# Two key weight loads moved to ScalarE's DMA queue, and two value weight loads moved ahead of the fifth token tile's load

## The chip, the cores and the metric

The kernel runs on one core of a Trainium2 chip. The metric is device time in microseconds (us) of one execution. A kernel's executions agree to a few tenths of a per cent, so every ratio is given with its 95% interval. The "span" of a profile runs from its first to its last instruction and is about 1.7 us shorter than the time of the same execution.

## The reference, cut to what matters

```python
x = A_x                                       # 2048 tokens of 448 numbers
h = x + A(layernorm(x), A_wqkv, A_w_phi, A_wo)
h2 = h + B(layernorm(h), B_w_gate, B_w_up, B_w_down)

def A(x, wqkv, w_phi, wo):                    # linear attention, 16 heads of 28
    q, k, v = split(x @ wqkv)
    pk = einsum("bhsd,hdf->bhsf", k, w_phi)   # the same w_phi for q
    ...
```

The kernel never forms k: it multiplies the key weights by w_phi once (the "fold") and projects each normalised token tile with the product. So the first projection needs three things: token tiles 0 and 1, normalised and transposed; all key weights; and w_phi. The value weights are needed one step later.

## The kernel before

Every operation has a name, and for each engine a string gives the order in which that engine runs its operations. Waits on semaphores are worked out from what the operations read and write.

```python
ORDER = {
    "sp":  "x1 x0 ld_k0 x2 ld_k2 x4 x6 ld_v0 x10 ld_v2 ld_q2 x8 ld_q3 ..."       # cut
    "act": "wphi3 wphi2 wphi1 wphi0 wTe1 wTe0 wTe3 w2e0_0 w2e0_1 w2e0_2 w2e0_3 xn3 ..."
    "pe":  "warm0 wT1 wT0 warm1 xT1 warm2 xT0 warm3 wT2 wT3 w2m0_0 warm4 w2m0_1 "
           "w2m0_3 w2m0_2 warm5 xT2 warm6 ppa0 warm7 ppb0 xT3 vva0 vvb0 ppa2 ..."
    "dve": "zero bd0 bst1 agg1 bst0 agg0 ve1_0 nm1_0 nm1_1 xn1 bst2 bst3 agg2 agg3 ve1_3 "
           "xT0e wTe2 bst5 nm1_3 bst4 agg5 agg4 bst6 xT1e ve1_4 ..."
    "pool": "... ve1_1 pow1_1 pow1_0 xn0 v1ones mask1 nm1_2 ve1_2 pow1_2 nb1_2 xn2 ..."
}
# ... cut ...
def kload(a, b):      # two of the four key weight blocks, 196 KB
    load("ld_k%d" % a, wk_sb[:, a:b, :], A_wqkv[a * GP:b * GP, D:2 * D]..., [...], (b - a) * 98)
# ... cut ...
load("wphi%d" % hl, Wphi[...], ..., [("Wphi", hl)], 6, r=["Wphi"], eng="act")    # after bd0 zeroed the tile
```

`x1` and `x0` load one token tile each (112 KB), `x2`, `x4`, `x6`, ... two tiles each (224 KB); `ld_v0` and `ld_v2` are the value weights (224 KB each). `bst` are a tile's statistics on VectorE (DVE), `xn` the normalisation, `xT` its transposition on TensorE (PE), `xTe` the copy out of PSUM. `wT` transposes key weights, `w2m0` is the fold (the key weights by w_phi) and `w2e0` its copies; `ppa0` is the first key projection and `vva0` the first value projection. The `warm` groups are multiplications of zeros that fill TensorE until data comes.

The softmax here doesn't subtract the row's maximum and nothing guards it: scores larger than these inputs give would overflow.

Of the kernel before, what the change touches and what calls it, by code (L numbers as in the profile page):

```python
# [18 lines left out]
class Graph:  # L19
# [86 lines left out]
    def emit(self, nc):  # L106
# [94 lines left out]

ORDER = {
    "sp": (
        "x1 x0 ld_k0 x2 ld_k2 x4 x6 ld_v0 x10 ld_v2 ld_q2 x8 ld_q3 ld_q1 ld_q0 xT4 xT5 xT6 x14 x12 xT7 ld_woe1 xT8 "
        "xT9 xT10 xT11 xT12 xT13 xT14 ld_woo1 xT15 ld_wd0 ld_woe0 ld_wu2 ld_wg0 ld_wg2 ld_wd1 ld_wg3 ld_wu3 ld_woo0 "
        "ld_wu0 ld_wg1 ld_wd4 ld_wd6 ld_wu1 oT3 oT2 oT4 oT5 oT6 oT7 hT2 ld_wd3 ld_wd2 hT3 ld_wd5 hT4 oT8 oT9 hT5 hT6 "
        "hT7 oT11 oT10 oT12 out3 out1 hT9 hT8 oT13 hT11 hT10 oT14 oT15 out5 hT12 hT14 out2 hT15 out4 hT13 out9 out7 "
        "out10 out6 out14 out0 out15 out12 out11 out8 out13 "
    ),
    "act": (  # L210
        "wphi3 wphi2 wphi1 wphi0 wTe1 wTe0 wTe3 w2e0_0 w2e0_1 w2e0_2 w2e0_3 xn3 xn4 ek0 ek1 xn5 v1_0 v1_1 xn6 ek2 ek3 "
        "v1_2 w2e1_1 v1_3 xn7 ek4 w2e1_3 xn9 w2e1_2 ek5 v1_5 v1_6 ek6 xn11 ek7 xn12 ek8 v1_8 xn13 ek9 xn14 ek10 v1_10 "
        "ek11 v1_11 ek12 v1_12 ek13 v1_13 ek14 eq0_0 ek15 v1_14 v1_15 eq0_1 eq1_0 eq1_1 eq2_0 oT0e eq2_1 sq0 sq1 "
        "eq3_0 eq3_1 sig0_1 sig0_0 sig0_3 sig0_2 sig0_5 sig0_4 sig0_7 sq2 sig0_6 sq3 sig0_9 sig0_8 sig0_10 sig0_11 "
        "sq5 sig0_12 sig0_13 sq4 sq7 sig2_0 sig2_1 sq6 sig2_3 sig2_2 sig2_5 sig2_4 sig2_6 sig2_7 sig2_8 sig2_9 "
        "sig2_10 sig2_11 sig2_12 sig2_13 sig4_1 sq9 sig4_0 sig4_3 sq8 sig4_2 sig4_5 sig4_4 sig4_7 sig4_6 sig4_9 sq10 "
        "sig4_8 sq11 sig4_11 sig4_10 sig4_13 sig4_12 sig8_1 sig8_0 sq13 sig8_2 sig8_3 sig8_4 sig8_5 sq12 sig8_6 sq14 "
        "sq15 sig8_7 sig8_9 sig8_8 sig8_10 sig8_11 sig8_13 sig8_12 sig12_0 sig12_1 sig12_3 sig12_2 sig12_5 sig12_4 "
        "sig12_7 sig12_6 sig12_8 sig12_9 sig12_11 sig12_10 sig12_12 sig12_13 "
    ),  # L220
    "pe": (
        "warm0 wT1 wT0 warm1 xT1 warm2 xT0 warm3 wT2 wT3 w2m0_0 warm4 w2m0_1 w2m0_3 w2m0_2 warm5 xT2 warm6 ppa0 warm7 "
# [83 lines left out]
def build(nc, A_x, A_wqkv, A_w_phi, A_wo, B_w_gate, B_w_up, B_w_down, out):  # L306
# [10 lines left out]
    with ExitStack() as es:  # L317
# [69 lines left out]
        def load(name, dst, src, w, kb, r=(), eng="sp"):  # L387
            return op(eng, name, lambda e: e.dma_start(dst, src), r=r, w=w, dma="in" if eng == "sp" else "ain",  # L388
                      nring=48 if eng == "sp" else 8, kb=kb)
# [34 lines left out]

        def kload(a, b):
            load("ld_k%d" % a, wk_sb[:, a:b, :], A_wqkv[a * GP:b * GP, D:2 * D].rearrange("(kt p) n -> p kt n", p=GP),
                 [("wk", kt) for kt in range(a, b)], (b - a) * 98)

        def vload(k):
            r0 = ROW0[k]  # L430
            load("ld_v%d" % k, wv_sb[:, k:k + 2, :], A_wqkv[r0:r0 + 256, 2 * D:3 * D].rearrange("(kt p) n -> p kt n", p=P),
                 [("wv", k), ("wv", k + 1)], 224)
        kload(0, 2)
        kload(2, 4)
        for hl in range(4):
            load("wphi%d" % hl, Wphi[hl * DH:(hl + 1) * DH, :, hl * DH:(hl + 1) * DH],
# [98 lines left out]
        for kt in range(KT):  # L535
            b = (0, 1, 4, 5)[kt]
# [351 lines left out]
```

## Time and profile before

| | before |
|---|---|
| time, median of 3 runs | 208.53 us (207.93 to 208.68) |
| span of the profiled run | 206.8 us |
| TensorE busy | 199.2 us, 96% of the span |
| first key projection starts | 10.59 us |

Three lines of the page of the kernel before: busy time, share and instructions of each engine, and the shares of the chain that ended last, by engine and by line.

```profile
PE 199.2 (96%) x2457; PEld 112.6 (54%) x2457; DVE 136.6 (66%) x343; ACT 95.2 (46%) x185; POOL 59.0 (29%) x99
...
PE 86%; DVE 4%; POOL 3%; DMA 2%; issue 1%; ACT 1%; SPq 1%
PE psum L289 79%; PE psum L814 5%; DMA x_sb<-in_A_x_dram 2%; POOL o_pad L700 1%; PE psum L478 1%; POOL rst L728 1%; SPq L388 1%; DVE hn_pad L732 1%; DVE st L485 1%; ACT eq L637 0%; PE psum L553 0%; ACT eq L638 0%; POOL xn_pad L514 0%; PE psum L464 0%; DVE hhT L788 0%
```

TensorE bounds the kernel: it is busy for 96% of the span and carries 86% of the chain.

Stretches of the span of the same kernel (columns: length, then the busy time and count of PE, of its weight loads, of DVE, ACT and POOL, the granted clock, the DMA share and rate):

```profile
0.00:10.59 10.59, 9.15 (x86) 6.02 (x87) 7.33 (x26) 4.56 (x8) 6.64 (x24) 1.00 0.84 225
...
13.00:30.00 17.00, 16.80 (x232) 9.63 (x230) 16.53 (x36) 16.54 (x35) 14.57 (x18) 1.00 0.44 98
...
100.00:150.00 50.00, 49.99 (x526) 24.14 (x522) 31.87 (x77) 18.89 (x39) 7.59 (x18) 1.00 0.22 43
```

In the first 10.59 us TensorE counts as busy for 9.15 us, but most of that is zeros. From 13 us on it has nearly no gap, so whatever delays the first projection should delay the end.

TensorE's timeline of the head (start us, duration, engine, line, operation, tiles, count; in brackets the idle time before it and what ended it):

```profile
1.24 4.02 PE L464 MATMUL psum<-zero 128*128 128x512 bf16 x9 [1.24 <-DVE zero L392]
5.22 0.99 PE L540 MATMUL psum<-ident,wk_sb 112*112 112x112 bf16 x8
...
6.90 0.39 PE L478 MATMUL psum<-ident,xn_pad 128*128 128x128 bf16 x4
...
7.59 0.36 PE L553 MATMUL psum<-Wphi,WkT 112*128 112x112 bf16 x4
...
9.76 0.40 PE L478 MATMUL psum<-ident,xn_pad 128*128 128x128 bf16 x4 [0.20 <-POOL xn_pad L514]
...
10.59 0.93 PE L289 MATMUL psum<-Wk,xnT 64*128 64x448 bf16 x8
...
12.73 1.55 PE L289 MATMUL psum<-wv_sb,xnT 64*128 64x448 bf16 x12
```

(The last row counts only what starts before 14 us, the end of the window.) These are, in order: the first warm-up group, the first key transposes, tile 0's transpose, the first fold group, tile 2's transpose, the first key projection and the first value projection. The only stop between them is 0.20 us, for tile 2's normalisation on GpSimd (POOL).

VectorE's timeline of the same stretch: statistics of tile 1, of tiles 2 and 3, of tile 5, then the copy of tile 1's transpose, without which the first projection cannot start:

```profile
2.88 0.63 DVE L485 BATCH_NORM_STATS2 st<-x_sb 128x6 f32<-128x448 bf16 x1 [1.46 <-DMA x_sb<-in_A_x_dram]
...
6.05 1.15 DVE L485 BATCH_NORM_STATS2 st<-x_sb 128x6 f32<-128x448 bf16 x2 [0.58 <-DMA x_sb<-in_A_x_dram]
...
8.15 0.62 DVE L485 BATCH_NORM_STATS2 st<-x_sb 128x6 f32<-128x448 bf16 x1
...
10.00 0.41 DVE L471 COPY xnT<-psum 128x512 bf16<-128x512 bf16 x1
```

The first of them waited for tile 1 (landed 2.1 us after its issue at 0.79), the second for tiles 2 and 3. The piece of the chain of waits that stands for the load of tiles 2 and 3 (start us, length, what):

```profile
2.17 3.85 DMA x_sb<-in_A_x_dram
```

From there the chain runs over VectorE's statistics and over GpSimd to tile 2's normalisation, which ends at 9.71 us, just before tile 2's transpose.

### The profile page before, as it was taken

How to read it: one execution, taken by the hardware profiler on the slowest of the kernel's cores; microseconds unless marked ns; L12 is line 12 of the kernel's file. 1: busy time of each engine (PE TensorE's matmuls, PEld its weight loads, DVE VectorE, ACT ScalarE, POOL GpSimd, SP SyncE). 2: the span in 40 equal slices, each digit the busy share in tenths (PEclk: the TensorE clock that was granted, in tenths of full speed). 3: DMA queues.
4: the chain of work that ended last, by engine and by line, in shares of the span. 5: the costliest groups of instructions: out<-in, count | busy, mean ns of one | idle time of the engine just before them, and what ended most of it. 6: DMA issues, size and time to landing. Idle time of an engine off the chain costs nothing.

```text
span 206.8 us, 5794 instructions
## 1 busy us (share of the span) xinstructions
PE 199.2 (96%) x2457; PEld 112.6 (54%) x2457; DVE 136.6 (66%) x343; ACT 95.2 (46%) x185; POOL 59.0 (29%) x99
## 2 busy tenths in 40 slices
PE   7999999999989999999999999999999999999991
PEld 2935666775446666777444444444555555544450
DVE  4899999978899897767768967446332513353151
ACT  2689999878792536222333342324323122122100
POOL 4868999831345404400032020001400000000000
PEclk9999999999999999999999999999999999999997
DMA  5945344899122270413005411030321000020013
GB/s 156 292 107 135 82 95 88 247 382 258 56 51 54 44 166 32 79 25 55 3 0 91 109 29 25 15 41 22 78 49 25 3 0 3 0 89 3 0 37 119
DMA packets 32722, 16.25 MB, mean 79 GB/s; under 512 B 24952, under 2 KB 31800, under 8 KB 32696
## 3 DMA queue, kind: packets, MB, share of 16 engines
q1 hardware_dynamic: 32192, 15.86, 31.2%
q8 instruction: 19, 0.31, 0.6%
q10 hardware_dynamic: 504, 0.03, 0.2%
q14 instruction: 7, 0.06, 0.1%
HBM read 8.34 MB, written 1.84 MB: 49 GB/s over the span
## 4 chain that ended last, share of the span: by engine, by line
PE 86%; DVE 4%; POOL 3%; DMA 2%; issue 1%; ACT 1%; SPq 1%
PE psum L289 79%; PE psum L814 5%; DMA x_sb<-in_A_x_dram 2%; POOL o_pad L700 1%; PE psum L478 1%; POOL rst L728 1%; SPq L388 1%; DVE hn_pad L732 1%; DVE st L485 1%; ACT eq L637 0%; PE psum L553 0%; ACT eq L638 0%; POOL xn_pad L514 0%; PE psum L464 0%; DVE hhT L788 0%
## 5 line engine op out<-in xcount | busy, mean ns | idle before, releaser
L289 PE MATMUL psum<-xnT,wg_sb 64*128 64x512 bf16 (+1 forms) x490 | 94.6, 333 | 0.7 <-DVE qq L685 0.6
L289 PE MATMUL psum<-xnT,wu_sb 64*128 64x512 bf16 (+1 forms) x490 | 94.5, 334 | 0.3
L787 ACT ACTIVATE sg_sb<-psum 128x512 bf16<-128x512 f32 (+1 forms) x70 | 35.0, 512 | 89.9 <-PE psum L289 89.4
L788 DVE SCALAR_TENSOR_TENSOR hhT<-sg_sb,psum 128x512 bf16<-128x512 bf16 (+1 forms) x70 | 39.1, 576 | 50.8 <-ACT sg_sb L787 50.3
L289 PEld LDWEIGHTS psum<-xnT,wg_sb 64*128 64x128 bf16 x490 | 43.8, 94 | 23.7 <-DVE hhT L788 4.8
L289 PEld LDWEIGHTS psum<-xnT,wu_sb 64*128 64x128 bf16 x490 | 43.9, 94 | 15.1 <-PE psum L289 1.4
L289 PE MATMUL psum<-wd_sb,hhT 64*128 64x448 bf16 x336 | 37.2, 349 | 0.0
L289 PEld LDWEIGHTS psum<-wd_sb,hhT 64*128 64x128 bf16 x336 | 17.3, 94 | 14.8 <-DVE x_sb L718 0.6
L607 POOL TENSOR_TENSOR phi<-hhT,rs 128x896 bf16<-128x896 bf16 x13 | 22.7, 1770 | 2.6 <-DVE rs L604 1.5
L289 PE MATMUL psum<-wv_sb,xnT 64*128 64x448 bf16 x112 | 22.0, 350 | 0.1
L289 PE MATMUL psum<-Wk,xnT 64*128 64x448 bf16 x112 | 22.0, 350 | 0.1
L726 POOL TENSOR_SCALAR ve<-ssq 128x1 f32<-128x1 f32 x16 | 3.1, 192 | 61.2 <-ACT junk L723 60.4
L603 DVE TENSOR_REDUCE ss<-hhT 128x32 f32<-128x896 bf16 x16 | 17.0, 1070 | 1.2 <-ACT hhT L600 1.1
L700 POOL TENSOR_TENSOR o_pad<-c_sb,rden 128x448 bf16<-128x448 bf16 x12 | 11.2, 937 | 19.0 <-DVE rden L695 17.4
L289 PE MATMUL psum<-xnT,Wq 64*120 64x512 bf16 x112 | 14.7, 381 | 0.2
L289 PE MATMUL psum<-wo_e,oT 64*128 64x448 bf16 x56 | 13.2, 350 | 0.2 <-DVE oT L471 0.2
L289 PE MATMUL psum<-wo_o,oT 64*128 64x448 bf16 x56 | 13.2, 350 | 0.1
L289 PEld LDWEIGHTS psum<-v,phi 64*120 64x120 bf16 x256 | 10.9, 131 | 3.3 <-PE psum L289 0.2
L821 DVE SCALAR_TENSOR_TENSOR x_sb<-psum,x_sb 128x448 bf16<-128x448 f32 x16 | 9.4, 619 | 3.5 <-PE psum L814 3.1
L723 ACT ACTIVATE junk<-x_sb,nm 128x448 bf16<-128x448 bf16 x16 | 10.6, 663 | 2.2 <-DVE nm L721 2.1
L289 PE MATMUL psum<-v,phi 64*120 64x116 bf16 x256 | 11.1, 213 | 0.1
L814 PE MATMUL psum<-wd_sb,hhT 128*128 128x448 bf16 x56 | 11.1, 353 | 0.0
(82 smaller groups left out, 240.2 us busy)
## 6 DMA issues: line engine op xcount, KB each, us to landing
out_dram<-x_sb SPq DMA_DIRECT2D x16, 112.0 KB, 1.8
x_sb<-in_A_x_dram SPq DMA_DIRECT2D x7, 224.0 KB, 4.3
wd_sb<-in_B_w_down_dram SPq DMA_DIRECT2D x7, 224.0 KB, 4.1
wg_sb<-in_B_w_gate_dram SPq DMA_DIRECT2D x3, 448.0 KB, 6.6
wu_sb<-in_B_w_up_dram SPq DMA_DIRECT2D x3, 448.0 KB, 9.9
wv_sb<-in_A_wqkv_dram SPq DMA_DIRECT2D x2, 224.0 KB, 4.8
wk_sb<-in_A_wqkv_dram SPq DMA_DIRECT2D x2, 196.0 KB, 3.9
wo_e<-in_A_wo_dram SPq DMA_DIRECT2D x1, 336.0 KB, 3.4
```

Source lines behind the costliest of these rows:

```text
L289: p = e.matmul(o, lhsT=w, rhs=r, start=st, stop=sp, tile_position=(row, 0))
L388: return op(eng, name, lambda e: e.dma_start(dst, src), r=r, w=w, dma="in" if eng == "sp" else "ain", nring=48 if eng == "sp" else 8, kb=kb)
L478: p = e.transpose(ps[:, kt * P:(kt + 1) * P], src, ident[:])
L603: op("dve", "ss%d" % t, lambda e: e.tensor_reduce(ss[:, s, :], eks, AX.X, ALU.add), r=[("ek", s)], w=[("ss", s)])
L607: return e.tensor_tensor(phi[:, sp, :, :, :].rearrange("p a g (f n) -> p (a g f) n", f=2)[:, :, 0:56].rearrange("p b (h d) -> p b h d", h= ...
L700: return e.tensor_tensor(o_pad[:, so, off:off + D].rearrange("p (h d) -> p h d", h=H), c_sb[:, s, :, 0:DH], rden[:, s, :][:, :, None].to_b ...
L723: op("act", "sq%d" % t, lambda e: e.activation(junk[:, t % 2, :], h_sb[:, t, :], ACT.Square, bias=nm2[:, t:t + 1], accum_out=ssq2[:, t:t + ...
L726: op("pool", "ve%d" % t, lambda e: e.tensor_scalar(ve2[:, t:t + 1], ssq2[:, t:t + 1], 1.0 / D, EPS, op0=ALU.mult, op1=ALU.add), r=[("ssq2" ...
L787: op("act", "sig" + nm, lambda e: e.activation(sg_sb[:, k, 0:N], bk(bg)[:, 0:N], ACT.Tanh, scale=0.5), r=[B(bg)], w=[("sg", k)])
L788: op("dve", "hh" + nm, lambda e: e.scalar_tensor_tensor(out=hhT[(t0 // 4) % NHH][:, ff, ns], in0=sg_sb[:, k, 0:N], scalar=1.0, in1=bk(bu)[ ...
L814: p = e.matmul(bk(b)[:, 0:D], lhsT=hb[:, ff, TS(t)], rhs=wd_sb[:, ff, :], start=ff == 0, stop=ff == FT - 1)
L821: op("dve", "fin%d" % t, lambda e: e.scalar_tensor_tensor(out=h_sb[:, t, :], in0=bk(b)[:, 0:D], scalar=0.5, in1=h_sb[:, t, :], op0=ALU.mul ...
```

## The change

Its intent: start the key weights, which several steps follow, at once on a second queue; and use the room on SyncE's queue to bring the value weights earlier. The diff, cut to its core (the rest only re-wraps the order strings):

```diff
 ORDER = {
     "sp": (
-        "x1 x0 ld_k0 x2 ld_k2 x4 x6 ld_v0 x10 ld_v2 ld_q2 x8 ..."
+        "x1 x0 x2 ld_v0 ld_v2 x4 x6 x10 ld_q2 x8 ..."
     "act": (
-        "wphi3 wphi2 wphi1 wphi0 wTe1 ..."
+        "ld_k0 ld_k2 wphi3 wphi2 wphi1 wphi0 wTe1 ..."
 ...
         def kload(a, b):
             load("ld_k%d" % a, ...,
-                 [("wk", kt) for kt in range(a, b)], (b - a) * 98)
+                 [("wk", kt) for kt in range(a, b)], (b - a) * 98, eng='act')
```

## The prediction

> **What bounds the kernel now.** TensorE. The busy table gives it 199.2 of 206.8 us, and the chain that ended last runs through it for 86% of the span. The change touches only the first 11 us. There, the stretch table has the DMA engines full from 2 to 12 us (share 0.86 to 1.16), so loads are limited by bytes, not by issue. TensorE is filled with zero warm-up matmuls (first group 1.24 to 5.26 us); its only real stop in the head after the start is 0.20 us at 9.76, before tile 2's transpose. The first projection starts at 10.59 us; from 13 us on TensorE is busy at 16.8 of 17 us, so a shift of that start should pass nearly whole into the span.
>
> **What ends just before 10.59.** Three near ties in the timeline: the warm-up group after tile 2's transpose (until about 10.6), the last folded-key-weight copy on ScalarE (10.10), tile 1's transposed copy on VectorE (10.41). Value weights landed 4.8 us after issue, near 10 us, and their first matmul is at 12.73: 2.7 us of slack. Key weights: the first transposes start at 5.22 us when the warm-up group ends, the second ones at 7.18 behind token tile 0's transpose. So almost nobody waits for the hastened loads.
>
> **What moves.**
> - Removed: two issues of 0.43 us from SyncE before tiles 2-3's load. It goes out 0.47 us earlier (2.17 to 1.70). It landed at 6.02.
> - Added: the same two issues on ScalarE before the four w_phi issues (1.93 us together from 1.45), which slip about 0.9 us; the table load after them (3.41) slips but ends before ScalarE's first copy at 5.88.
> - The Trainium skill (DMA: Bandwidth & Descriptors, "Queues, rings and completion order") says each DMA engine takes turns between queues, packet by packet on the same 16 DMA engines. So 392 KB of key weights now compete from the first microsecond with tiles 1 and 0 (112 KB each, landed near 2.9 and 3.8 us). At the measured 210 to 235 GB/s of 2 to 4 us, 112 KB of rival traffic is 0.5 us. Estimate: tile 1 +0.5, tile 0 +0.5 to +0.9 us; tiles 2-3 about unchanged.
> - w_phi, 6 KB each in tiny packets, now sits behind the key weights in ScalarE's queue. Estimate: last landing from before 7.5 to about 7.5-8.3 us, and the fold needs it at 7.54.
> - Tiles 4-5 and 6-7 get 448 KB of value weights ahead of them: at the 309 to 365 GB/s of 6 to 9 us that is 1.2 to 1.5 us. VectorE takes their statistics (8.15 and 9.49 us) before tile 1's transposed copy, which the first projection needs.
>
> **Critical path.** Gain: at most the 0.20 us stop. Loss: VectorE's in-order queue and the fold slip 0.3 to 1 us, so the first projection starts near 11.1 instead of 10.59. Little later slack absorbs it (stops of 0.56 and 0.19 us at 61 and 54 us).
>
> **Predicted:** 208.9 us, 8 in 10 between 208.0 and 210.0. Faster by over 2%: 0.02; within 2%: 0.96; slower by over 2%: 0.02.
>
> **What would show it.** First tile's statistics later than 2.88 us; tile 0's transpose later than 6.90; first projection later than 10.59; tile 4-5 statistics waiting on their load; w_phi wait before the fold; value weights earlier without anybody starting sooner.
>
> **What would make it wrong.** If ScalarE's queue starts late or gets less than half the turns, tiles 0 and 1 are not delayed, and 2-3 arrive early: gain up to 0.2 us or slightly more. If two queues move more than one, the head shortens. If the tightly ordered middle (13 to 75 us) re-synchronises, the shift may grow or vanish.

## More of the kernel before

GpSimd's timeline, tile 2's normalisation:

```profile
8.94 0.77 POOL L514 TENSOR_SCALAR xn_pad<-x_sb,nm,rst 128x512 bf16<-128x512 bf16 x1
```

## The result, and the profile after

The changed kernel took 209.0 us (median of 4, 208.91 to 209.37) against 208.42 us for the kernel before (median of 4). The ratio is 1.0034, with a 95% interval of 1.0011 to 1.0057. Ratios here are the mean time of one kernel's fast runs over the mean of the other's fast runs of the same rounds, so they are not quite the quotient of the medians. The change is inside 2%, and it is a small loss: 0.6 us by the medians, 0.7 us by the ratio.

The same three lines of the page of the changed kernel:

```profile
PE 199.0 (96%) x2457; PEld 112.1 (54%) x2457; DVE 136.9 (66%) x343; ACT 95.3 (46%) x185; POOL 58.9 (28%) x99
...
PE 85%; DMA 5%; DVE 3%; POOL 2%; ACT 1%; ACTq 1%; issue 1%
PE psum L289 77%; PE psum L814 5%; DMA Wphi<-in_A_w_phi_dram 2%; DMA oT<-o_pad 2%; ACTq L388 1%; PE psum L553 1%; POOL o_pad L700 1%; PE psum L464 1%; POOL rst L728 1%; PE psum L478 1%; DVE hn_pad L732 1%; ACT eq L637 0%; ACT eq L638 0%; DVE hhT L788 0%; ACT sg_sb L787 0%
```

TensorE's work is the same, and a piece of the chain has gone to w_phi's load and to a transposing DMA (oT). Stretches of the changed kernel:

```profile
13.00:30.00 17.00, 16.80 (x225) 9.50 (x224) 16.34 (x36) 16.52 (x35) 14.53 (x18) 1.00 0.50 94
...
100.00:150.00 50.00, 49.66 (x520) 24.09 (x518) 32.45 (x79) 18.55 (x38) 7.56 (x18) 1.00 0.21 41
```

The stretch from 13 to 30 us has the same 16.80 us of TensorE work as before. From 100 to 150 us TensorE lost 0.33 us (49.66 instead of 49.99).

TensorE's timeline: first key transposes, tile 0's transpose, first fold group, tile 2's transpose, first key projection, first value projection.

```profile
5.05 0.89 PE L540 MATMUL psum<-ident,wk_sb 112*112 112x112 bf16 x8
...
7.23 0.40 PE L478 MATMUL psum<-ident,xn_pad 128*128 128x128 bf16 x4 [0.34 <-POOL xn_pad L514]
...
8.39 0.36 PE L553 MATMUL psum<-Wphi,WkT 112*128 112x112 bf16 x4 [0.30 <-DMA Wphi<-in_A_w_phi_dram]
...
10.13 0.39 PE L478 MATMUL psum<-ident,xn_pad 128*128 128x128 bf16 x4
...
10.95 0.93 PE L289 MATMUL psum<-Wk,xnT 64*128 64x448 bf16 x8
...
13.09 0.93 PE L289 MATMUL psum<-wv_sb,xnT 64*128 64x448 bf16 x8
```

VectorE's timeline: statistics of tile 1, of tiles 2 and 3, of tile 5, and the copy of tile 1's transpose.

```profile
3.65 0.63 DVE L485 BATCH_NORM_STATS2 st<-x_sb 128x6 f32<-128x448 bf16 x1 [2.22 <-DMA x_sb<-in_A_x_dram]
...
6.07 1.14 DVE L485 BATCH_NORM_STATS2 st<-x_sb 128x6 f32<-128x448 bf16 x2
...
8.30 0.62 DVE L485 BATCH_NORM_STATS2 st<-x_sb 128x6 f32<-128x448 bf16 x1
...
10.14 0.41 DVE L471 COPY xnT<-psum 128x512 bf16<-128x512 bf16 x1
```

GpSimd's timeline, tile 2's normalisation:

```profile
9.29 0.77 POOL L514 TENSOR_SCALAR xn_pad<-x_sb,nm,rst 128x512 bf16<-128x512 bf16 x1
```

Two pieces of its chain of waits: the last w_phi load and a late transposing DMA.

```profile
3.28 4.98 DMA Wphi<-in_A_w_phi_dram
...
109.65 4.55 DMA oT<-o_pad
```

What to read there. Tile 1's statistics start at 3.65 us instead of 2.88, waiting for its load. Tile 0's transpose moves from 6.90 to 7.23. The fold stops for 0.30 us, and the last w_phi load ends that stop: it is now what the chain runs through, in place of the load of tiles 2 and 3. The first projection starts at 10.95 instead of 10.59, 0.36 us later. The value weights land at 6.7 and 7.4 us (issue plus time to landing), which were 8.8 and 10.0 us, and the first value projection starts 0.36 us *later*. Nobody was waiting for them.

The chain shows one path only, and here a second one ended level with it. GpSimd ended tile 2's normalisation at 10.05 us, 0.08 us before tile 2's transpose, so without the wait for w_phi that transpose could have started hardly earlier. GpSimd's path hangs on tile 0: the first projection came 6.41 to 6.43 us after tile 0's landing in all four runs where the keys go at once and tiles 4 and 5 are in time (the change, c0, e1, e8), with a wait for w_phi (the change, c0) and without one (e1, e8). Tile 0's normalisation on GpSimd moved by 0.68 us (5.72 to 6.40), tile 2's by only 0.35, because in the kernel before GpSimd had stood idle for 0.39 us between the two, until the statistics of tile 2 were there.

The other part of the longer span comes at 110 us, where one transposing DMA of the attention output took 4.55 us to land.

Landings read from the two profiles, issue time plus time to landing (us):

| load | before | after |
|---|---|---|
| tile 1 | 2.9 | 3.6 |
| tile 0 | 3.8 | 4.5 |
| key weights, first and second half | 5.2, 7.0 | 4.2, 5.3 |
| tiles 2 and 3 | 6.0 | 5.9 |
| tiles 4 and 5 | 7.5 | 8.1 |

### The profile page after: what moved, and what is told of

Same layout as the page of the kernel before. It is cut to its first block, busy times and chain, and to the rows that moved or that the text cites. A ratio compares the mean times of both kernels' runs of the same rounds, so it can differ in the third digit from the quotient of the medians.

```text
span 207.6 us, 5794 instructions
## 1 busy us (share of the span) xinstructions
PE 199.0 (96%) x2457; PEld 112.1 (54%) x2457; DVE 136.9 (66%) x343; ACT 95.3 (46%) x185; POOL 58.9 (28%) x99
## 4 chain that ended last, share of the span: by engine, by line
PE 85%; DMA 5%; DVE 3%; POOL 2%; ACT 1%; ACTq 1%; issue 1%
PE psum L289 77%; PE psum L814 5%; DMA Wphi<-in_A_w_phi_dram 2%; DMA oT<-o_pad 2%; ACTq L388 1%; PE psum L553 1%; POOL o_pad L700 1%; PE psum L464 1%; POOL rst L728 1%; PE psum L478 1%; DVE hn_pad L732 1%; ACT eq L637 0%; ACT eq L638 0%; DVE hhT L788 0%; ACT sg_sb L787 0%
## 5 line engine op out<-in xcount | busy, mean ns | idle before, releaser
L723 ACT ACTIVATE junk<-x_sb,nm 128x448 bf16<-128x448 bf16 x16 | 10.6, 663 | 2.0 <-DVE nm L721 1.9
L289 PE MATMUL psum<-v,phi 64*120 64x116 bf16 x256 | 11.1, 213 | 0.1
L814 PE MATMUL psum<-wd_sb,hhT 128*128 128x448 bf16 x56 | 11.1, 353 | 0.0
```

What stands on the lines that cost most here:

```text
L289: p = e.matmul(o, lhsT=w, rhs=r, start=st, stop=sp, tile_position=(row, 0))
L723: op("act", "sq%d" % t, lambda e: e.activation(junk[:, t % 2, :], h_sb[:, t, :], ACT.Square, bias=nm2[:, t:t + 1], accum_out=ssq2[:, t:t + ...
L814: p = e.matmul(bk(b)[:, 0:D], lhsT=hb[:, ff, TS(t)], rhs=wd_sb[:, ff, :], start=ff == 0, stop=ff == FT - 1)
```

## The experiments

Twelve kernels ran on three chips, each timed in five rounds (up to six runs, counting the profiled one) beside the kernel before, and all gave correct results. The diffs of e1 to e3 are against the full change; for the others it is said.

| run | first statistics, us | first projection, us | span, us | ratio to before (95% interval) |
|---|---|---|---|---|
| before (its own profile) | 2.88 | 10.59 | 206.8 | 1 |
| the change (its own profile) | 3.65 | 10.95 | 207.6 | 1.0034 (1.0011 to 1.0057) |
| c0 the change again | 3.71 | 11.09 | 207.3 | 1.0021 (1.0003 to 1.0040) |
| e1 keys only | 3.82 | 11.21 | 207.4 | 1.0021 (1.0007 to 1.0035) |
| e2 values only | 2.93 | 11.44 | 207.8 | 1.0032 (1.0015 to 1.0049) |
| e3 w_phi before keys | 2.87 | 16.56 | 213.2 | 1.0287 (1.0261 to 1.0313) |
| e4 w_phi on SyncE | 3.73 | 11.46 | 207.7 | 1.0053 (1.0037 to 1.0068) |
| e5 e4, keys later | 2.96 | 11.59 | 208.0 | 1.0062 (1.0042 to 1.0083) |
| e6 e2, copy first | 2.91 | 10.42 | 206.9 | 1.0016 (1.0001 to 1.0032) |
| e7 before, w_phi on SyncE | 2.92 | 10.05 | 206.3 | 0.9999 (0.9983 to 1.0015) |
| e8 keys at once, rest tidy | 4.03 | 11.37 | 208.4 | 1.0026 (1.0000 to 1.0052) |
| e9 e8, keys 0.66 us later | 2.90 | 10.69 | 207.3 | 1.0006 (0.9983 to 1.0029) |
| e10 before, late head | 2.91 | 10.48 | 207.2 | 1.0010 (0.9984 to 1.0036) |
| e11 short head | 2.87 | 9.82 | 206.3 | 0.9993 (0.9967 to 1.0019) |

A profile shows one execution, and not always a typical one. Those of the change (209.37 us) and of e8 (210.15) are of the slowest of their runs, those of e7 (208.03) and e11 (208.01) of the fastest.

My first theory (A) was that the key loads on the second queue make the loss, in two ways: they compete with the first token tiles, and they stand ahead of w_phi. The first rival (B) was that the value loads make it, by delaying tiles 4 and 5, whose statistics VectorE takes before it copies tile 1.

### c0: the change once more

No edit.

> The changed kernel once more, unaltered, as the control of this batch. My theory: the loss is a late head (first key projection at 10.95 us in the profile instead of 10.59) plus a late wait near 114 us that may be chance. Expect a ratio to the kernel before of 1.002 to 1.005, first projection at 10.9 to 11.0 us. If the stall of 0.33 us on an oT transpose near 114 us is part of the change it comes again; if it was chance, the span is nearer +0.4 us.

The loss came again in a second set of runs, ratio 1.0021. TensorE's timeline, fold and first projection:

```profile
8.46 0.36 PE L553 MATMUL psum<-Wphi,WkT 112*128 112x112 bf16 x4 [0.22 <-DMA Wphi<-in_A_w_phi_dram]
...
11.09 0.93 PE L289 MATMUL psum<-Wk,xnT 64*128 64x448 bf16 x8
```

The wait for w_phi is there again (0.22 us). The late transposing DMA near 110 us is not: the span was 207.3 instead of 207.6 although the first projection was later. So that part of the first difference was most likely chance and not the change. GpSimd ended tile 2's normalisation at 10.20 us and tile 2's transpose started at 10.25: here the wait for w_phi cost nothing.

### e1: only the key loads move

```diff
-  "sp": "x1 x0 x2 ld_v0 ld_v2 x4 x6 x10 ..."
+  "sp": "x1 x0 x2 x4 x6 ld_v0 x10 ld_v2 ..."
```

> Only the key weight loads go to ScalarE's queue; value weights stay where the kernel before has them among the tile loads. Theory A (the competing key loads and the w_phi loads stuck behind them make the loss): same as the full change, ratio 1.002 to 1.005, first projection about 10.95 us, w_phi landing about 8.2 us. Rival B (the value loads ahead of tiles 4 to 7 make the loss through VectorE's statistics): as before, ratio 1.000, first projection about 10.6 us.

As theory A had it: ratio 1.0021, first projection 11.21. But the wait for w_phi was gone. TensorE's first fold group (no bracket, so no stop):

```profile
8.40 0.36 PE L553 MATMUL psum<-Wphi,WkT 112*128 112x112 bf16 x4
```

The chain of waits ran through tile 0's load and GpSimd instead:

```profile
1.24 3.56 DMA x_sb<-in_A_x_dram
```

So the delay of tiles 1 and 0 alone is enough for the loss. The head has three arms: the fold with w_phi, VectorE with tile 1's copy, and GpSimd with tile 2's normalisation. The wait for w_phi belongs to an arm that happened to end level with GpSimd's.

### e2: only the value loads move

```diff
-  "sp": "x1 x0 x2 ld_v0 ld_v2 x4 x6 x10 ..."
+  "sp": "x1 x0 ld_k0 x2 ld_k2 ld_v0 ld_v2 x4 x6 x10 ..."
-  "act": "ld_k0 ld_k2 wphi3 ..."          # and kload without eng='act'
+  "act": "wphi3 ..."
```

> Only the value weight loads go ahead of tile 4's load; the key weight loads stay on SyncE's queue where they were. Theory A: within 0.1 % of the kernel before, first projection 10.6 us, first statistics at 2.9 us, w_phi ready before 7.5 us. Rival B: VectorE waits for tiles 4-5 from 8.15 us to about 8.8, tile 1's copy at about 10.6, first projection about 10.8 to 11.0, ratio 1.002 to 1.004.

Here theory A was wrong and rival B right: ratio 1.0032. VectorE's statistics of tile 5, with the wait ahead of it, and the copy of tile 1:

```profile
9.03 0.63 DVE L485 BATCH_NORM_STATS2 st<-x_sb 128x6 f32<-128x448 bf16 x1 [0.75 <-DMA x_sb<-in_A_x_dram]
...
10.89 0.41 DVE L471 COPY xnT<-psum 128x512 bf16<-128x512 bf16 x1
```

TensorE's first projection, which waited for that copy (the bracket names VectorE; the instruction it names is the neighbour of the copy that ended at 11.30):

```profile
11.44 0.93 PE L289 MATMUL psum<-Wk,xnT 64*128 64x448 bf16 x8 [0.73 <-DVE ve L493]
```

Tile 1 is on time (2.93 us), but tiles 4 and 5 land at 9.0 us and VectorE stands still for 0.75 us in front of an operation that TensorE needs. In the full change this does not occur: there the key loads have left SyncE's queue, the load of tiles 4 and 5 is issued at 3.16 us (3.14 before), lands at 8.1, and VectorE is busy until 8.30 anyway. Each half of the change costs something alone, and the two costs do not add: the first projection was 0.62 us late with the keys alone, 0.85 with the values alone, and 0.36 and 0.50 with both, against the one profile of the kernel before. The times of this set say the same: 1.0021 and 1.0032 alone, 1.0021 together (c0).

### e3: w_phi ahead of the keys on ScalarE's queue

```diff
-  "act": "ld_k0 ld_k2 wphi3 wphi2 wphi1 wphi0 ..."
+  "act": "wphi3 wphi2 wphi1 wphi0 ld_k0 ld_k2 ..."
```

> The full change, but ScalarE issues the four w_phi loads ahead of its key weight loads; w_phi waits for the zeroing of its tile until 1.42 us, so the key loads go out at about 3.4 and 3.8 us, after tiles 1 and 0 have their turns. Theory A: tiles 1 and 0 land as before (statistics near 2.9 us), w_phi no longer awaited at 8.3; key weights land later, first key transposes perhaps at 5.6 instead of 5.05. First projection 10.5 to 10.75, ratio 0.999 to 1.002. If neither the competition at 1.8 to 4 us nor w_phi's place is the cause, the first projection stays near 10.95 and the ratio at 1.003.

A plain miss: ratio 1.0287, a loss of 6 us. Tile 1 was on time as expected, but the key loads, issued at 3.44 and 3.87 us, took 6.7 and 7.6 us to land (3.5 and 4.4 in the kernel before). TensorE's first key transposes:

```profile
10.14 0.99 PE L540 MATMUL psum<-ident,wk_sb 112*112 112x112 bf16 x8 [5.17 <-DMA wk_sb<-in_A_wqkv_dram]
```

And a stretch of it:

```profile
10.50:13.00 2.50, 2.50 (x28) 2.50 (x26) 0.33 (x1) 0.96 (x2) 0.00 (x0) 0.50 0.94 224
```

After the stop TensorE also ran at a granted clock of 0.50. What went wrong in my expectation: I took no account of what already stood in the queues. By 3.44 us SyncE had issued 1,120 KB and ScalarE's own queue held the small w_phi packets; the keys had to wait behind the second, and, as I read it, to share turns with the first. The trace's records have the first key packet at 5.76 us, just as the w_phi packets of its queue ran out (the last at 5.80).

### e4: w_phi on SyncE's queue

```diff
-  "sp": "x1 x0 x2 ld_v0 ..."                       # of the full change
+  "sp": "x1 x0 x2 wphi3 wphi2 wphi1 wphi0 ld_v0 ..."
-  load("wphi%d" % hl, ..., r=["Wphi"], eng="act")
+  load("wphi%d" % hl, ..., r=["Wphi"])
```

> The full change, but the four w_phi loads go on SyncE's queue after tiles 2-3, so they no longer stand behind the key weights. Theory now (three arms): the first projection starts when the last of three arms ends: the fold arm (w_phi and key weights), VectorE's arm (tiles 1, 0, 2-3, 4-5, 6 in order, then tile 1's copy) and GpSimd's arm (tile 2's normalisation). The changed kernel loses on two arms at once: its fold waits 0.22 to 0.30 us for w_phi, and tiles 1 and 0 are late by 0.8 us. Expect: no wait for w_phi, first statistics still near 3.7, first projection 10.85 to 11.05 us, ratio to before 1.001 to 1.003, so nearly no gain over the change. Rival (w_phi's place alone is the cause): first projection back to 10.6 and ratio 1.000.

The wait for w_phi was gone and the first statistics were late (3.73), as expected. That w_phi's place alone was not the cause can be read from tile 2's transpose, which comes ahead of what spoilt the rest: it started at 10.32 us without any wait for w_phi, and at 10.13 in the change with one. But the first projection was later still, 11.46, and the ratio 1.0053. The reason is in the chain of waits:

```profile
4.92 4.10 DMA x_sb<-in_A_x_dram
```

That is the load of tiles 4 and 5. The four w_phi issues took 1.73 us on SyncE and pushed it from 3.16 to 4.92. So I had built rival B's delay into the test of theory A.

### e5: e4 with the key loads 0.66 us later

```diff
-  [("wk", kt) for kt in range(a, b)], (b - a) * 98, eng='act')
+  [("wk", kt) for kt in range(a, b)], (b - a) * 98, r=['Wphi'], eng='act')   # waits for bd0
```

> As e4, and ScalarE's two key loads wait for the zeroing of w_phi's tile, so they go out at about 1.46 us instead of 0.79: tile 1 has the DMA engines to itself for most of its transfer. Three arms: first statistics at 2.9 to 3.1 us, tile 0 about 4.0, first key transposes still near 5.2, first projection 10.55 to 10.75, ratio 0.999 to 1.001. If the early competition is not the cause, first projection stays at 10.9 to 11.0.

VectorE's timeline, statistics of tiles 1 and 5:

```profile
2.96 0.63 DVE L485 BATCH_NORM_STATS2 st<-x_sb 128x6 f32<-128x448 bf16 x1 [1.54 <-DMA x_sb<-in_A_x_dram]
...
9.18 0.63 DVE L485 BATCH_NORM_STATS2 st<-x_sb 128x6 f32<-128x448 bf16 x1 [0.98 <-DMA x_sb<-in_A_x_dram]
```

The first statistics came back to 2.96 us, so the competition does what theory A says. The first projection did not come back, because VectorE again waited for tiles 4 and 5. The run shows one arm and is spoilt for the time; e8 and e9 repeat it without that fault.

### e6: e2 with tile 1's copy ahead of the statistics

```diff
-  "dve": "... wTe2 bst5 nm1_3 bst4 agg5 agg4 bst6 xT1e ..."
+  "dve": "... wTe2 xT1e bst5 nm1_3 bst4 agg5 agg4 bst6 ..."
```

> The value-only kernel of e2 (whose first projection waited for VectorE until 11.44 us), but VectorE copies tile 1's transpose before the statistics of tiles 4, 5 and 6. Three arms: the late tile 4-5 load no longer stands between tile 1 and the first projection, which starts at 10.6 to 10.75 us; ratio to before 1.000 to 1.001 although the loads are exactly those of e2 (1.0032). If tile 4-5's lateness hurts by another way, the ratio stays near 1.003.

With the loads of e2, this order starts the first projection at 10.42 us instead of 11.44. That confirms the way in which late tiles 4 and 5 hurt: through VectorE's order, not through data that TensorE lacks. TensorE's first projection and the third key projection group:

```profile
10.42 0.93 PE L289 MATMUL psum<-Wk,xnT 64*128 64x448 bf16 x8
...
14.54 1.74 PE L289 MATMUL psum<-Wk,xnT 64*128 64x448 bf16 x14 [0.24 <-ACT hhT L600]
```

The ratio fell to 1.0016, more than the expected 1.000 to 1.001, though the interval reaches down to 1.0001; it overlaps that of e2, so the gain is shown at the first projection and not in the times. A new stop of 0.24 us on ScalarE at 14.54 us may have taken part of the gain back.

### e7: the kernel before with w_phi on SyncE's queue

```diff
-  "sp":  "x1 x0 ld_k0 x2 ld_k2 x4 ..."
+  "sp":  "x1 x0 ld_k0 x2 ld_k2 wphi3 wphi2 wphi1 wphi0 x4 ..."
-  "act": "wphi3 wphi2 wphi1 wphi0 wTe1 ..."       # and eng="act" taken from the load
+  "act": "wTe1 ..."
```

> The kernel before, with only the w_phi loads moved to SyncE's queue behind the key weights, so that one queue alone moves everything. It tests whether the small w_phi packets of the second queue, taking turns, slow tiles 0 to 3 in the kernel before. If they do: tile 2-3 lands at 5.0 to 5.6 instead of 6.0, first projection 10.4 to 10.6 (the warm-up groups and VectorE's order hold the rest), ratio 0.998 to 1.000. If not: tile 2-3 lands at 6.0, ratio 1.000.

Tiles 2 and 3 landed at 5.1 us instead of 6.0, and the first projection started at 10.05. The times did not follow: 0.9999. One profile of each kernel is too little here, and that of e7 is of its fastest run. The loads of e11 are those of e7, and there the statistics of tiles 2 and 3 began at 5.60, not 5.20; the loads of e10 are those of the kernel before, and there they began at 5.54, not 6.05. Whether w_phi's small packets slow the big loads by a few tenths stays open.

### e8 and e9: the early competition alone

e8, against the full change:

```diff
-  "sp": "x1 x0 x2 ld_v0 ld_v2 x4 x6 x10 ..."
+  "sp": "x1 x0 x2 x4 wphi3 wphi2 wphi1 wphi0 x6 ld_v0 x10 ld_v2 ..."     # w_phi without eng="act"
```

> Key loads on ScalarE at once (as in the change), value loads back among the tiles, w_phi on SyncE's queue after tiles 4-5, so neither w_phi nor tile 4-5 is the last to come (e4 and e5 were spoilt by w_phi's 1.73 us of issue time standing ahead of tiles 4-5). Only the early competition is left. Expect first statistics at about 3.7 us, no wait for w_phi or tiles 4-5, first projection 10.9 to 11.2 us, ratio 1.002 to 1.004.

e9, against e8:

```diff
-  [("wk", kt) for kt in range(a, b)], (b - a) * 98, eng='act')
+  [("wk", kt) for kt in range(a, b)], (b - a) * 98, r=['Wphi'], eng='act')
```

> e8 with one difference: the key loads wait for the zeroing of w_phi's tile and are issued at 1.46 us instead of 0.79. Competition theory: first statistics at about 2.95 us, first projection 10.3 to 10.6, about 0.6 us earlier than e8; ratio 0.998 to 1.001, clearly under e8's. If the competition for the first tiles is not what delays the head, e8 and e9 come out alike.

VectorE's first statistics in e8, then TensorE's first projection in e8:

```profile
4.03 0.63 DVE L485 BATCH_NORM_STATS2 st<-x_sb 128x6 f32<-128x448 bf16 x1 [2.61 <-DMA x_sb<-in_A_x_dram]
```

```profile
11.37 0.93 PE L289 MATMUL psum<-Wk,xnT 64*128 64x448 bf16 x8
```

The same two for e9, with its first key transposes ahead of the projection:

```profile
2.90 0.63 DVE L485 BATCH_NORM_STATS2 st<-x_sb 128x6 f32<-128x448 bf16 x1 [1.48 <-DMA x_sb<-in_A_x_dram]
```

```profile
5.54 0.62 PE L540 MATMUL psum<-ident,wk_sb 112*112 112x112 bf16 x8 [0.28 <-DMA wk_sb<-in_A_wqkv_dram]
...
10.69 0.93 PE L289 MATMUL psum<-Wk,xnT 64*128 64x448 bf16 x8
```

The only difference is when the first of the two key loads is issued, at 0.79 or 1.45 us; the second follows it. Issued at once, they delay tile 1's statistics by 1.13 us and the first projection by 0.68 us. e9's projection was just above its expected 10.3 to 10.6, since TensorE now stopped for late keys (0.28 and 0.31 us) and for w_phi (0.20 us). The times agree in direction, 1.0026 and 1.0006, but their intervals overlap: the effect is shown at the first projection, not in the times of this pair, and e8's profile is of its slowest run.

### e10: a late head with the loads of before

```diff
-  for i, (n, size) in enumerate((..., (9, 128), (9, 128), (3, 128))):
+  for i, (n, size) in enumerate((..., (9, 128), (16, 128), (3, 128))):
```

> The kernel before with all its loads as they were and only seven more of the 128-column warm-up matmuls just ahead of the first projection (each about 0.055 us, so 0.39 us). It measures what a later first projection costs by itself. If the span follows the first projection one to one: first projection at about 10.97 us, ratio 1.0015 to 1.0022, the loss of the changed kernel without its loads. If the tail absorbs it: 1.000.

The added zeros took 0.39 us (that group lasted 1.06 instead of 0.67 us), yet the first projection started at 10.48, not 10.97, and the ratio 1.0010 is not told apart from 1. The projection missed because the loads themselves came 0.5 us earlier in this execution (statistics of tiles 2 and 3 at 5.54 instead of 6.05). Without the added group it would have started near 10.09, by subtraction. Four kernels have the same loads up to tiles 2 and 3, and the statistics of these tiles began at 6.05 (before), 6.10 (e2), 5.88 (e6) and 5.54 us (e10). So the 10.59 of the one profile of the kernel before lies towards the late end of a scatter of about 0.5 us, and e10 at the early one.

### e11: towards a shorter head

```diff
   # e7, and
-  "dve": "... wTe2 bst5 ... bst6 xT1e ..."
+  "dve": "... wTe2 xT1e bst5 ... bst6 ..."
-  ... (9, 128), (9, 128), (3, 128)
+  ... (9, 128), (3, 128), (3, 128)
```

> Towards a faster version: e7 (w_phi behind the key weights on one queue; first projection 10.05) with tile 1's copy ahead of tile 4 to 6's statistics and six warm-up matmuls fewer before the first projection. If the head passes one to one: first projection 9.65 to 9.85 us, ratio 0.995 to 0.997. e7 gained 0.5 us at the first projection in its profile and nothing in its times, so the rival is that something after the head (statistics, copies, value loads that come at 11 us) takes it back: ratio 0.998 to 1.000.

TensorE's first projection, and the third key projection group:

```profile
9.82 0.93 PE L289 MATMUL psum<-Wk,xnT 64*128 64x448 bf16 x8
...
13.91 1.74 PE L289 MATMUL psum<-Wk,xnT 64*128 64x448 bf16 x14 [0.22 <-ACT hhT L600]
```

The first projection started at 9.82 us, the earliest of all, as expected. A stop of 0.22 us on ScalarE followed, the profile is of the fastest run, and the ratio was 0.9993, with 1 well inside the interval. The rival of that expectation held: no version here is shown to beat the kernel before.

### Does the span follow the first projection?

Span minus start of the first projection was 196.2 to 196.4 us in seven of the fourteen profiles (before, c0, e1, e2, e4, e5, e7), whose first projections lie between 10.05 and 11.59. It was 196.5 in e6 and e11, which had the stop on ScalarE; 196.6 to 196.7 in the change's own profile, e3, e9 and e10, where a transposing DMA of the attention output took 4.4 to 4.6 us to land and the chain of waits ran through it; and 197.0 in e8, whose chain had two such late transposes. So a later first projection passes to the end one to one, and a chance event of about 0.4 us lies on top. Of the same kernel, the change's own profile had it and c0 had not. What makes a transpose late was not settled; in all five profiles that have it near 110 us (115 in e3) the issue of the next transpose took 2.35 to 2.62 us on SyncE, where the median is 1.26.

## Why the prediction was right, point by point

The prediction gave 208.9 us between 208.0 and 210.0, and the measured time was 209.0. Its ground, early competition that makes the head late and a late head that passes to the end, held better than its path. That the number came out right was in part luck: of the two arms that it blamed, VectorE's behind tiles 4 and 5 did not decide, and the fold's only ended level with a third, GpSimd's, from which it had expected at most a gain.

- **TensorE bounds it, and the start of the first projection passes nearly whole into the span.** Right: the remainder above is constant to about 0.2 us, apart from the chance event and the ScalarE stop.
- **The key loads have almost nobody waiting for them.** Right: they landed 1.0 and 1.8 us earlier (4.2 and 5.3 us) and the first key transposes, behind the warm-up group, started at 5.05 instead of 5.22.
- **Tiles 1 and 0 late by 0.5 and 0.5 to 0.9 us.** Right in kind: measured about 0.7 for each at landing, 0.77 at the first statistics. In all five profiles with the keys issued at once on the second queue the first statistics came at 3.65 to 4.03 us (the change, c0, e1, e4, e8); in the nine others at 2.87 to 2.96. This agrees with the Trainium skill (DMA: Bandwidth & Descriptors, "Queues, rings and completion order"), by which each DMA engine takes turns between queues: from 2 to 3 us of the change SyncE's queue moved 0.09 MB in 120 packets and ScalarE's 0.10 MB in 114. e9 against e8 shows that it is the competition.
- **w_phi last landing 7.5 to 8.3 us.** Right: the chain has it at 8.26, and the fold waited 0.30 us (0.22 in c0). But by GpSimd's arm the first projection would have come nearly as late without it.
- **Tiles 4 and 5 late by 1.2 to 1.5 us.** Wrong: 0.5 us (8.1 against 7.5), and VectorE did not wait. This is the term that was mis-sized. e2, where the keys stay on SyncE's queue, has what I had reckoned (9.0, so 1.5 us). The bytes up to and with tiles 4 and 5, keys included, are the same 1,512 KB in both, but with the keys on a second queue this load was issued at 3.16 and not at 4.16 us, and it landed 1.0 us sooner; both kernels took 4.9 us from its issue to its landing. The reckoning had taken the rate of the kernel before as given, but from 3 to 7 us the DMA engines moved 315 GB/s in the change and 236 in e2 (270 and 294 in the kernel before and e10, whose loads are the same). So "limited by bytes, not by issue" did not hold as it stood. Whether the second queue, the earlier issue or chance moved more was not separated.
- **The head's slip of 0.3 to 1 us, with the first projection near 11.1.** Right in size: 10.95 and 11.09. The path was only partly right: the prediction let VectorE and the fold share the blame. VectorE's copy of tile 1 ended at 10.55, 0.4 us before the projection; the fold arm with w_phi and GpSimd's arm behind tile 0 ended level in the change, and GpSimd's alone gives the same delay in e1 (11.21) and e8 (11.37).
- **The 0.20 us stop before tile 2's transpose is the most that can be gained.** The stop did disappear, and brought nothing, because the fold arm and GpSimd's own were later.

Of what was named as able to make it wrong, the ordered middle absorbed nothing, and tiles 4 and 5 came sooner with two queues than with e2's one, without a shorter head. The size of the loss is known only roughly: 0.34% and 0.21% in two sets of runs, with one profile of the kernel before, whose head scatters by 0.5 us.

## What to carry to other kernels

Before moving a load to a second queue, ask which loads land first today and who waits for them: the second queue gives its bytes a share at once, and takes it from the loads that the start of the chain hangs on. Then follow every arm that ends near the same time, not only the one that the chain shows: here the arm that decided was GpSimd's, behind tile 0. Ask too what stands behind it in its new queue, and what already stands in the queues when it is issued; tiny loads behind big ones, and big ones behind tiny ones, both came late here. And in a head with several arms that end within some tenths of a microsecond of each other, halves of a change need not add, and a test of one arm is worth nothing until the other arms are kept from ending later.

## What the Trainium skill lacked or had wrong

- DMA: Bandwidth & Descriptors, "Issuing engines are not separate DMA queues", says that issuing from several engines only saves the sequencer's time. It says that the transfers interleave, but not what that costs: the loads at the head of the other queue came late (tile 1 landed at 3.6 us instead of 2.9). Whether the sequencer's time is all that is saved stays open: tiles 4 and 5 landed 1.0 us sooner in the change than in e2, with the same bytes before them, and the runs do not tell why.
- The same page, "Queues, rings and completion order", describes the turns but not what they do to a big load that is put behind many tiny packets while the other queue has a backlog: the key loads of e3 took 6.7 and 7.6 us to land, against 3.5 and 4.4 in the kernel before.
- No page that I found tells that a transposing DMA sometimes comes late by chance: 4.4 to 4.6 us to landing where the median is 2.5, in five of fourteen profiles (near 110 us, 115 in e3), about 0.4 us of span each time; of the same kernel, one profile had it and another had not.
